# Batch 0's half-way feature: a product with ones before the first chunk in place of one-row products in its first four steps

## Chip, core and metric

One core of a Trainium2 chip runs the kernel. It has TensorE (matrix products; PE, with its weight loads as PEld), VectorE (DVE), ScalarE (ACT), GpSimd (POOL) and SyncE (SP, which here only issues transfers). The metric is the device time of one execution in microseconds (us). All numbers are float32.

## What is computed

The input `x` has 8 batches of 3136 rows by 256 features. The first part is a Fourier mixing: an FFT along the rows, an FFT along the features, and of the result the real part. The second is a gated feed-forward layer with a short convolution:

```python
X = np.fft.fft(x, axis=1); X = np.fft.fft(X, axis=2); x = X.real
h = np.maximum(x @ w_in, 0.0)                       # 256 -> 1024
conv_out = sum over k of conv_w[k] * hp[:, k:k + S] # 3 taps along the rows, h padded by zeros
gate = 1.0 / (1.0 + np.exp(-conv_out))
return h * gate @ w_out                             # 1024 -> 256
```

Cosine and sine tables of the FFT along the rows are an input too. The weights arrive as 64-bit numbers and are narrowed on the chip.

## The kernel before

**The mixing.** The FFT along the rows is made by products with the tables. By symmetry, rows n and S - n and features d and D - d are folded together first (`fold_ops`, VectorE), so that a batch needs half the outputs. For each batch nine small *units* (`units`) multiply the folded rows with the tables: TensorE makes two parts in one PSUM bank, ScalarE copies one part out (`copy`), and VectorE adds and subtracts the two (`fin`). The results are two tables per batch, `PQ[b][0]` (`pt`, the cosine side) and `PQ[b][1]` (`qt`, the sine side), with 128 partitions of features and 1569 columns of frequencies.

**The feature D/2.** Feature 128, the half-way one, is its own mirror image, and its row of the cosine side has no place among the 128 partitions of `pt`. It is kept as a row `er` of 1569 values on one partition. For batch 0 the row comes in two parts. `row()` (L360) fetches the last partition of `qt`, which holds its odd columns, by a transfer. The unit `feature()` (L327) computes the even ones: its `copy` is four ScalarE copies of one row (L345), its `fin` is four GpSimd sums of one row (L353, L354). `flip()` (L364, ScalarE) then changes the sign of every fourth column. `store()` (L368) writes `er` to a row of the DRAM tensor `ed`, and `spread()` (L463) reads it back from there to all 128 partitions, one tile `eb[b, c]` for each chunk `c`; the pool of `eb` has four buffers. For the other batches another route (`Feature`, L374) fills `ed`.

**The weights.** The FFT along the features is put into the weight: `blocks(i)` (L614) multiplies the feature tables `dm` by a quarter `w4[i]` of `w_in` and has ScalarE copy the two results to `G[:, 0]` (cosine side) and `G[:, 1]` (sine side). For quarters 0 and 1 it also makes the one row of weights that belongs to feature D/2, and puts it into partition 0 of the tile `left` (L626, L627). `column(i)` (L631) makes that same row of weights as a column `ge`, one value for each of the 128 output channels of a block.

**The steps.** The 1024 channels are 8 blocks `f` of 128, the 1569 frequencies are 4 chunks `c` (`CUTS`). A step is `(b, c, f)`: 8 x 4 x 8 = 256 steps. For a step,

- `seed` (L660) lets ScalarE write `eb * ge[f]` into the PSUM tile `pa` (L668): the feature D/2. TensorE then adds to it without starting the bank anew.
- `products` (L680) makes `pb` from `G[:, 1]` and `qt`, and adds the product of `G[:, 0]` and `pt` to `pa`. In steps 3 to 19 (`triple`) a third product, of `G[:, 1]` and `qt`, is added to `pa` too.
- `copies` (L691, ScalarE) brings `pb` to SBUF (`nb`); in `triple` steps ScalarE also makes one half of `h` from `pa` (L699).
- `combine` (L704, VectorE) makes `h` (both halves by L713, in `triple` steps one), `first_tap` (L716, ScalarE), `other_taps` (L721, VectorE, L725), `sigmoid` (L734, ScalarE) and `gate` (L740, shared by GpSimd L745 and VectorE L746) follow in later cycles, and `mm2` (L750) multiplies the gated `h` by `w_out` into four PSUM banks `po` that are shared with the blocks and units (`spare`).

In the first four steps, `first(s)` is true (`FIRST = 4`): `seed` does nothing, and `products` adds the feature D/2 by a third TensorE product with one row on each side:

```python
if first(s):
    mm(pa[s][:, 0:n], left[0:1, f, :], er[b][:, ch.k0:ch.k1], False, not triple(s))
```

In steps 4 and 5, each the first seeded one in its `pa` bank, `start_all` (L667) makes a product over all 512 columns of the bank ahead of the seed. There are two `pa` banks, one `pb` bank and one bank `pd` for the units.

**The order.** It is written out by hand. Each engine executes its instructions in the order of the program text and waits in that order. Ahead of the steps come, for batch 0: `keep_on(16)` (L775), 16 products of 256 columns into an unused tile while the folds and the tables are on the way; the four odd units, quarter by quarter; `mend_row(0)` (L229), which scales one row of a table; the units 2, 4, 3, 7, 8, of which number 4 is `feature()`; `flip`, `store`, `spread` of all four chunks; the loads of half of batch 1; `blocks(0)`. SyncE's queue carries the row transfer, the load of `w_out`, the store, the spreads and the loads, in this order. Then, with `products` and `copies` of step 0 done, cycle `t` of the main loop (L901) issues: `sigmoid` of step t-2; a piece of weight narrowing ("first"); `products` and `copies` of step t+1; `combine` of step t; the other piece of the narrowing ("dve"); `seed` of step t+2; `first_tap` of t; `other_taps` of t-1; `gate` of t-2; loads ("load"); `mm2` of t-3; and what is placed at "pe". There, cycles 0, 1 and 2 hold `blocks(1)`, `blocks(2)` and `blocks(3)`, the last two with their columns, and cycles 0 and 1 also `column(0)` and `column(1)`. Narrowing is VectorE work with a power made by ScalarE in between (L525, then L527 on ScalarE, then L539, L540, L533, L543). In cycle 5, `Feature.place` takes the buffer of `er` for other tables, which gathers of 4-byte elements (L418) fill.

Of the kernel before, what the change touches and what calls it, by code (L numbers as in the profile page):

```python
# [9 lines left out]
F32 = mybir.dt.float32  # L10
I32 = mybir.dt.int32
U32 = mybir.dt.uint32
AF = mybir.ActivationFunctionType
# [14 lines left out]


TRIPLE = 3, 20  # L30
FIRST = 4
RC = 56
NQ = 8
CUTS = (0, 384, 768, 1152)
# [4 lines left out]
def kernel(  # L39
# [10 lines left out]
    nc = tc.nc  # L50
    B, S, D = x.shape
    F = moe_w_in.shape[1]
    P = 128
    M = S // 2
    Q4 = S // 4
    NP = Q4 // NQ
# [13 lines left out]
    const = ctx.enter_context(tc.tile_pool(name="const", bufs=1))  # L70
# [4 lines left out]
    ebp = ctx.enter_context(tc.tile_pool(name="ebp", bufs=4))  # L75
# [7 lines left out]
    psa = ctx.enter_context(tc.tile_pool(name="psa", bufs=2, space=PSUM))  # L83
    psb = ctx.enter_context(tc.tile_pool(name="psb", bufs=1, space=PSUM))
    psd = ctx.enter_context(tc.tile_pool(name="psd", bufs=1, space=PSUM))
# [5 lines left out]
    act = nc.scalar.activation  # L91

    def mm(o, l, r, start, stop):
        nc.tensor.matmul(o, l, r, start=start, stop=stop, skip_group_check=True)  # L94

    def spare():

        return pso.tile([P, 2, D], F32, name="po", tag="po").rearrange("p a d -> p (a d)")
# [4 lines left out]
    xh, wt, ea = {}, {}, {}  # L103
# [101 lines left out]
    PQ, eb, er = {}, {}, {}  # L205
# [29 lines left out]
    def mirror_tables(q):  # L235

        for to, of, s in ((2, 1, -1.0), (3, 0, 1.0)):
            for i in range(2):
                act(tabs[1][0:KR, to, q:q + 2, i:HO:2], tabs[1][0:KR, of, q:q + 2, i:HO:2], AF.Copy,
                    scale=-s if i else s)  # L240
# [222 lines left out]
    def spread(b, cs):  # L463

        for c in cs:
            ch = chunks[c]
            eb[b, c] = ebp.tile([P, HN], F32, name="eb", tag="eb")[:, 0:ch.k1 - ch.k0]
            nc.sync.dma_start(out=eb[b, c], in_=ed[b:b + 1, ch.k0:ch.k1].to_broadcast([P, ch.k1 - ch.k0]))
# [31 lines left out]
    chunks = [Chunk(c) for c in range(len(CUTS))]  # L500
    HW = max(c.w for c in chunks)
    HN = max(c.k1 - c.k0 for c in chunks)
    left = const.tile([P, NF, P], F32, name="left")
# [42 lines left out]
    class Weight:  # L546
# [19 lines left out]
        def narrow(self, c0, c1):  # L566
            for f in self.parts(c0, c1):
                f()

    ident = gp.tile([3 * NF, 3 * NF], F32, name="ident", tag="g")  # L570
    make_identity(nc, ident)
    cw24 = gp.tile([3 * NF, 1, P], F32, name="cw24", tag="g")
# [10 lines left out]
    dm = gp.tile([P, 2, 2, P], F32, name="dm", tag="g")  # L583
    N4 = F // 4
    w4 = [win[i // 2][:, :, i % 2 * N4:(i % 2 + 1) * N4] for i in range(4)]
# [24 lines left out]
    G = const.tile([P, 2, F], F32, name="G")  # L610
    ge = const.tile([P, NF], F32, name="ge")
    cw = const.tile([P, 3, NF], F32, name="cw")

    def blocks(i):  # L614


        w = w4[i]
        for g in range(2):
            p = spare()
            for t in range(2):  # L620
                mm(p[:, 0:N4], dm[:, t, g, :], w[:, t], t == 0, t == 1)
            nc.scalar.copy(out=G[:, g, i * N4:(i + 1) * N4], in_=p[:, 0:N4])
        if 2 * i < FIRST:
            p = spare()
            for t in range(2):
                mm(p[0:1, N4:2 * N4], dm[:, t, 1, P - 1:P], w[:, t], t == 0, t == 1)  # L626
            nc.scalar.copy(out=left[0:1, 2 * i:2 * i + 2].rearrange("p f i -> p (f i)"), in_=p[0:1, N4:2 * N4])  # L627
        if i > 1:
            column(i)

    def column(i):  # L631
        w, p = w4[i], spare()
        for m in range(NF // 4):
            for t in range(2):
                mm(p[:, m:m + 1], w[:, t, m * P:(m + 1) * P], dm[:, t, 1, P - 1:P], t == 0, t == 1)
        nc.scalar.copy(out=ge[:, i * NF // 4:(i + 1) * NF // 4], in_=p[:, 0:NF // 4])
# [7 lines left out]
    rows = out.rearrange("b s d -> (b s) d")  # L644
    hs, gs, pa, pb, po, nb = {}, {}, {}, {}, {}, {}

    def start_all(p, l, r):

        mm(p, l, r, True, True)

    def cut(s):
        b, c, f = s
        ch = chunks[c]
        return ch, ch.k1 - ch.k0, slice(f * P, (f + 1) * P)

    def first(s):

        return s[0:2] == (0, 0) and s[2] < FIRST

    def seed(s):  # L660

        b, c, f = s
        ch, n, fs = cut(s)
        pa[s] = psa.tile([P, 512], F32, name="pa", tag="pa")
        if not first(s):
            if s in ((0, 0, FIRST), (0, 0, FIRST + 1)):
                start_all(pa[s].rearrange("p (t n) -> p t n", t=2), dm[:, 0, 0], w4[0])  # L667
            act(pa[s][:, 0:n], eb[b, c], AF.Copy, scale=ge[:, f:f + 1])  # L668

    def triple(s):  # L670

        return s[0] == 0 and TRIPLE[0] <= s[1] * NF + s[2] < TRIPLE[1]

    def row_of(s):
        hs[s] = hp.tile([P, HW], F32, name="h", tag="h")
        w = chunks[s[1]].w
        if chunks[s[1]].zeros:
            nc.gpsimd.memset(hs[s][:, 0:w:w - 1], 0.0)

    def products(s):  # L680
        b, c, f = s
        ch, n, fs = cut(s)
        pb[s] = psb.tile([P, 512], F32, name="pb", tag="pb")
        mm(pb[s][:, 0:n], G[0:P - 1, 1, fs], PQ[b][1][0:P - 1, ch.k0:ch.k1], True, True)
        mm(pa[s][:, 0:n], G[:, 0, fs], PQ[b][0][:, ch.k0:ch.k1], first(s), not first(s) and not triple(s))
        if first(s):
            mm(pa[s][:, 0:n], left[0:1, f, :], er[b][:, ch.k0:ch.k1], False, not triple(s))
        if triple(s):
            mm(pa[s][:, 0:n], G[0:P - 1, 1, fs], PQ[b][1][0:P - 1, ch.k0:ch.k1], False, True)

    def copies(s):  # L691

        ch, n, fs = cut(s)
        p = pb.pop(s)
        nb[s] = nbp.tile([P, 2, HN], F32, name="nb", tag="nb")
        if triple(s):
            act(nb[s][:, 1, ch.cols], p[:, ch.cols], AF.Copy, scale=-2.0)
            row_of(s)
            act(hs[s][:, ch.front], pa[s][:, ch.fcols], AF.Relu)  # L699
        else:  # L700
            for i, cols in enumerate((ch.fcols, ch.cols)):
                act(nb[s][:, i, cols], p[:, cols], AF.Copy, scale=-1.0 if i else 1.0)  # L702

    def combine(s):  # L704

        ch, n, fs = cut(s)
        a, c = pa.pop(s), nb.pop(s)
        if not triple(s):
            row_of(s)
        h = hs[s]  # L710
        for i, (to, cols) in enumerate(((h[:, ch.front], ch.fcols), (h[:, ch.back][:, ::-1], ch.cols))):
            if i or not triple(s):
                nc.vector._custom_dve(TENSOR_ADD_SAT, out=to, in0=a[:, cols], in1=c[:, i, cols],  # L713
                                      s0=BIG, s1=0.0)
# [19 lines left out]
    def sigmoid(s):  # L734

        v, p, r = shares(s)
        for c in (slice(p.start, r.stop), v):
            act(gs[s][:, c], gs[s][:, c], AF.Sigmoid)  # L738
# [33 lines left out]
    taps()  # L772
    idle = psb.tile([P, 512], F32, name="pb", tag="pb")

    def keep_on(n):  # L775

        for _ in range(n):
            mm(idle[:, 0:2 * P], wt[0][1][0:NP, 1, 0], wt[0][1][0:NP, 0, 0:2], True, True)

    begin, us, row, flip, store = units(0)  # L780
    begin()
# [4 lines left out]

    odds = [us[j] for j in (0, 1, 5, 6)]
    w_in[0].narrow(0, 2)
    keep_on(16)
    mirror_tables(0)  # L790
    mend_row(1, half)
    mirror_tables(2)
# [10 lines left out]
                    w_out.load(nc.sync)  # L803
    mend_row(0, half)
    w_in[1].narrow(0, 2)
    for i, u in enumerate(us[j] for j in (2, 4, 3, 7, 8)):
        u.matmuls(0, 1)
        u.copy()
        u.fin()
    flip()  # L810
    store()
    spread(0, range(len(chunks)))
    for f in load_ops(1, 0, nc.sync):
        f()
    blocks(0)
# [5 lines left out]
    def at(cycle, where, fn):  # L821
        side.setdefault((cycle, where), []).append(fn)
# [6 lines left out]
    def shared(cycle, w, c):  # L829
        for where, fn in zip(("first", "dve"), w.parts(c, c + 2, room)):  # L830
            at(cycle, where, fn)

    shared(0, w_in[3], 0)
    for i in (0, 1):
        at(i, "pe", lambda i=i: column(i))
    for cycle, c in ((2, 0), (3, 2), (5, 4), (7, 6)):
        shared(cycle, w_out, c)
    for j, fn in enumerate(load_ops(1, 1, nc.sync)):
# [26 lines left out]
    for b in range(1, B):  # L865
        begin, us, *_ = units(b)
        us = us[0:4] + us[5:]
        c0, n = ends[b], per * b - 3 - ends[b]
# [12 lines left out]
    for b in range(1, B):  # L881
        ops = fold_ops(b)
        c0, n = ends[b - 1], ends[b] - ends[b - 1]
# [12 lines left out]
    n = len(steps)  # L896
    seed(steps[0])
    seed(steps[1])
    products(steps[0])
    copies(steps[0])  # L900
    for t in range(n + LAG):  # L901
        def run(where):
            for fn in side.get((t, where), []):
                fn()
        if 0 <= t - 2 < n:
            sigmoid(steps[t - 2])
        run("first")
        if t + 1 < n:
            products(steps[t + 1])
            copies(steps[t + 1])  # L910
        run("act")
        if t < n:
            combine(steps[t])
        run("dve")
        if t + 2 < n:
            seed(steps[t + 2])
        if t < n:
            first_tap(steps[t])
        if 0 <= t - 1 < n:
            other_taps(steps[t - 1])  # L920
        if 0 <= t - 2 < n:
            gate(steps[t - 2])
        run("load")
        if t >= LAG:
            mm2(steps[t - LAG])
        run("pe")
# [66 lines left out]
```

## Time and profile before

| | |
|---|---|
| time, median of 7 runs | 1214.5 us (1213.68 to 1215.8) |
| the profiled execution: time | 1215.09 us |
| the profiled execution: span of its records | 1213.3 us |
| busy TensorE / weight loads | 1184.0 / 906.7 us |
| busy VectorE / ScalarE / GpSimd | 1119.8 / 881.3 / 373.9 us |
| mean granted clock of TensorE | 0.999 |
| chain that ended last: TensorE, VectorE | 71%, 20% of the span |

The profile is of one execution, so its durations add up to its own span, and the time outside the span is the rest of its 1215.09 us. A row of the timeline gives start and duration in us, the engine (PE is TensorE's products, PEld its weight loads, SPq the transfers that SyncE issues), the line of the program, the operation, the tile written and the tiles read, shapes, a count, and in brackets how long the engine stood idle before it and what released it. Nearly all TensorE work is recorded under line 94, the helper `mm`, so it is told apart by its tiles. One float32 product appears as two records. A row of busy time by stretches gives the stretch, its length, then busy time with the count of instructions for PE, PEld, DVE, ACT and POOL, the granted clock, the share of the transfer engines and GB/s.

### The profile page before, as it was taken

How to read it: one execution, taken by the hardware profiler on the slowest of the kernel's cores; microseconds unless marked ns; L12 is line 12 of the kernel's file. 1: busy time of each engine (PE TensorE's matmuls, PEld its weight loads, DVE VectorE, ACT ScalarE, POOL GpSimd, SP SyncE). 2: the span in 40 equal slices, each digit the busy share in tenths (PEclk: the TensorE clock that was granted, in tenths of full speed). 3: DMA queues.
4: the chain of work that ended last, by engine and by line, in shares of the span. 5: the costliest groups of instructions: out<-in, count | busy, mean ns of one | idle time of the engine just before them, and what ended most of it. 6: DMA issues, size and time to landing. Idle time of an engine off the chain costs nothing.

```text
span 1213.3 us, 15439 instructions
## 1 busy us (share of the span) xinstructions
PE 1184.0 (98%) x4870; PEld 906.7 (75%) x4870; DVE 1119.8 (92%) x1689; ACT 881.3 (73%) x1837; POOL 373.9 (31%) x475
## 2 busy tenths in 40 slices
PE   4999999999999999999999999999999999999998
PEld 3676676777777777777777777777777777777776
DVE  7799999999999899999989999999998988899996
ACT  2477656777777777777777777777777777788884
POOL 5224534243233232424224242332222222222222
PEclk9999999999999999999999999999999999999999
DMA  9522233211131210202021020310001000110000
GB/s 227 190 20 87 81 33 103 61 53 47 34 94 44 67 40 19 89 26 76 31 80 58 1 80 27 94 40 26 27 1 53 31 26 27 46 34 27 26 27 31
DMA packets 70213, 66.30 MB, mean 55 GB/s; under 512 B 28123, under 2 KB 57827, under 8 KB 70131
## 3 DMA queue, kind: packets, MB, share of 16 engines
q1 hardware_dynamic: 64493, 52.18, 15.2%
q0 software_dynamic: 5120, 12.85, 3.4%
q8 instruction: 39, 0.64, 0.2%
q10 hardware_dynamic: 518, 0.28, 0.1%
q14 instruction: 43, 0.35, 0.1%
HBM read 39.53 MB, written 25.74 MB: 54 GB/s over the span
## 4 chain that ended last, share of the span: by engine, by line
PE 71%; DVE 20%; issue 4%; ACT 2%; DMA 1%; DVEq 0%; SPq 0%; ACTq 0%
PE po L94 44%; PE pb L94 10%; PE pa L94 10%; DVE g L725 7%; PE pd L94 6%; DVE h L713 3%; DVE g L746 3%; DVE xh L158 2%; ACT nb L702 1%; DVE xh L169 1%; DVE w L186 1%; DVE w L187 1%; DMA xh<-in_x_dram 0%; ACT g L738 0%; DVE xh L173 0%
## 5 line engine op out<-in xcount | busy, mean ns | idle before, releaser
L94 PE MATMUL po<-wout,g 128*128 128x256 f32 x3072 | 710.1, 381 | 8.1 <-DVE g L746 7.6
L94 PEld LDWEIGHTS po<-wout,g 128*128 128x128 f32 x3072 | 580.1, 190 | 160.5 <-DVE g L746 38.2
L725 DVE SCALAR_TENSOR_TENSOR g<-h,cw,g 128x770 f32<-128x770 f32 (+1 forms) x512 | 548.6, 1072 | 9.3 <-ACT g L719 0.2
L745 POOL TENSOR_TENSOR g<-g,h 128x385 f32<-128x385 f32 (+1 forms) x256 | 234.1, 915 | 760.7 <-ACT g L738 494.0
L738 ACT ACTIVATE g<-g 128x385 f32<-128x385 f32 (+2 forms) x512 | 244.2, 527 | 190.2 <-DVE g L725 189.7
L702 ACT ACTIVATE nb<-pb 128x386 f32<-128x386 f32 (+2 forms) x478 | 210.8, 493 | 86.1 <-PE pb L94 85.0
L713 DVE CUSTOM_DVE_ANT_0 h<-pa,nb 128x386 f32<-128x386 f32 (+2 forms) x495 | 257.1, 560 | 1.0 <-PE pa L94 1.0
L719 ACT ACTIVATE g<-h,cw 128x770 f32<-128x770 f32 (+1 forms) x256 | 243.2, 950 | 0.2 <-DVE h L713 0.2
L94 PE MATMUL pb<-qt,G 127*128 127x387 f32 (+2 forms) x512 | 212.7, 496 | 0.0
L94 PE MATMUL pa<-pt,G 128*128 128x387 f32 (+2 forms) x512 | 211.8, 494 | 0.0
L668 ACT ACTIVATE pa<-eb,ge 128x387 f32<-128x387 f32 (+2 forms) x252 | 151.5, 601 | 1.2 <-ACT ft L459 0.6
L94 PEld LDWEIGHTS pa<-pt,G 128*128 128x128 f32 x512 | 96.8, 189 | 73.6 <-issue 18.2
L746 DVE TENSOR_TENSOR g<-g,h 128x385 f32<-128x385 f32 (+1 forms) x256 | 146.2, 571 | 0.9 <-ACT g L738 0.9
L94 PE MATMUL pd<-tab,w 98*128 98x196 f32 (+3 forms) x448 | 126.7, 374 | 0.0
L133 POOL DMA_INDIRECT xh<-in_x_dram,idx x64 | 105.9, 1655 | 13.3 <-issue 9.2
L94 PEld LDWEIGHTS pb<-qt,G 127*128 127x128 f32 x512 | 93.9, 190 | 18.2 <-issue 1.9
L94 PEld LDWEIGHTS pd<-tab,w 98*128 98x128 f32 (+1 forms) x448 | 84.7, 191 | 12.3
L765 ACT COPY os<-po 128x256 f32<-128x256 f32 x196 | 57.6, 395 | 7.8 <-PE po L94 4.6
L158 DVE TENSOR_TENSOR xh<-xh 98x1020 f32<-98x1020 f32 (+1 forms) x32 | 40.7, 1278 | 3.3 <-DMA xh<-in_x_dram,idx 3.3
L169 DVE TENSOR_TENSOR xh<-xh 98x1024 f32<-98x1024 f32 (+1 forms) x32 | 41.3, 1292 | 0.1
L188 POOL COPY w<-xh 98x4 f32<-98x4 f32 (+1 forms) x32 | 20.3, 633 | 28.0 <-DVE xh L169 14.8
L291 DVE TENSOR_TENSOR qt<-as,pd 128x197 f32<-128x197 f32 (+1 forms) x14 | 7.2, 517 | 20.3 <-ACT as L287 20.3
(117 smaller groups left out, 385.4 us busy)
## 6 DMA issues: line engine op xcount, KB each, us to landing
out_dram<-os SPq DMA_DIRECT2D x192, 128.0 KB
xh<-in_x_dram SPq DMA_DIRECT2D x16, 784.0 KB
eb<-ed SPq DMA_DIRECT2D x16, 193.5 KB
tab<-dft_seq_dram SPq DMA_DIRECT2D x4, 589.5 KB
raw<-in_moe_w_in_dram SPq DMA_DIRECT2D x4, 512.0 KB
raw<-in_moe_w_out_dram SPq DMA_DIRECT2D x1, 2048.0 KB
eb<-ed SPq DMA_DIRECT2D x8, 209.0 KB
eb<-ed SPq DMA_DIRECT2D x8, 193.0 KB
```

The lines of the kernel that those rows point to most:

```text
L94: nc.tensor.matmul(o, l, r, start=start, stop=stop, skip_group_check=True)
L133: nc.gpsimd.indirect_dma_start(out=xh[b, h][0:NP, 7 - m].rearrange("p q d -> p (q d)"), out_offset=None, in_=bass.AP(tensor=x.tensor, offs ...
L158: vt(a[:, :, :, 1:D], a[:, :, :, 1:D], r[:, :, :, D - 1:0:-1], op=ALU.add)
L668: act(pa[s][:, 0:n], eb[b, c], AF.Copy, scale=ge[:, f:f + 1])
L702: act(nb[s][:, i, cols], p[:, cols], AF.Copy, scale=-1.0 if i else 1.0)
L713: nc.vector._custom_dve(TENSOR_ADD_SAT, out=to, in0=a[:, cols], in1=c[:, i, cols], s0=BIG, s1=0.0)
L719: act(gs[s], hs[s][:, 0:n], AF.Copy, scale=cw[:, 0, s[2]:s[2] + 1])
L725: stt(out=g, in0=h[:, k:k + n], scalar=cw[:, k, f:f + 1], in1=g, op0=ALU.mult, op1=ALU.add)
L738: act(gs[s][:, c], gs[s][:, c], AF.Sigmoid)
L745: gt(g[:, p], g[:, p], h[:, p], op=ALU.mult)
L746: vt(g[:, v], g[:, v], h[:, v], op=ALU.mult)
L765: nc.scalar.copy(out=osb[:, j % 2], in_=pt[:, j % 2])
```

## The change

The feature D/2 of chunk 0 reaches all partitions by a product: a row of 128 ones (`one`) as the stationary side and `er` as the moving side, into the bank `pd`, from where ScalarE copies it to `eb[0, 0]`. All steps are then seeded alike; `first`, `FIRST`, `start_all`, the one-row products and the one-row weights in `left` are gone. `column(0)` moves ahead of `blocks(0)` and `column(1)` to just after step 0's copies. The unit `feature()` goes first among the last five, with `flip`, `store` and the spread of chunks 1 to 3 directly behind it. `keep_on` now makes 8 products of 512 columns, six into the unused tile and one into each of the two `pa` banks.

```diff
+    one = const.tile([1, P], F32, name="one")
+    nc.gpsimd.memset(one, 1.0)
     ident = gp.tile([3 * NF, 3 * NF], F32, name="ident", tag="g")
...
-        if 2 * i < FIRST:
-            p = spare()
-            for t in range(2):
-                mm(p[0:1, N4:2 * N4], dm[:, t, 1, P - 1:P], w[:, t], t == 0, t == 1)
-            nc.scalar.copy(out=left[0:1, 2 * i:2 * i + 2].rearrange("p f i -> p (f i)"), in_=p[0:1, N4:2 * N4])
         if i > 1:
             column(i)
...
         pa[s] = psa.tile([P, 512], F32, name="pa", tag="pa")
-        if not first(s):
-            if s in ((0, 0, FIRST), (0, 0, FIRST + 1)):
-                start_all(pa[s].rearrange("p (t n) -> p t n", t=2), dm[:, 0, 0], w4[0])
-            act(pa[s][:, 0:n], eb[b, c], AF.Copy, scale=ge[:, f:f + 1])
+        act(pa[s][:, 0:n], eb[b, c], AF.Copy, scale=ge[:, f:f + 1])
...
-        mm(pa[s][:, 0:n], G[:, 0, fs], PQ[b][0][:, ch.k0:ch.k1], first(s), not first(s) and not triple(s))
-        if first(s):
-            mm(pa[s][:, 0:n], left[0:1, f, :], er[b][:, ch.k0:ch.k1], False, not triple(s))
+        mm(pa[s][:, 0:n], G[:, 0, fs], PQ[b][0][:, ch.k0:ch.k1], False, not triple(s))
...
-    def keep_on(n):
-
-        for _ in range(n):
-            mm(idle[:, 0:2 * P], wt[0][1][0:NP, 1, 0], wt[0][1][0:NP, 0, 0:2], True, True)
+    def keep_on(banks):
+
+        for p in banks:
+            mm(p.rearrange("p (s q d) -> p s q d", s=2, q=2), wt[0][1][0:NP, 1, 0], wt[0][1][0:NP, 0:2, 0:2],
+               True, True)
...
-    keep_on(16)
+    keep_on([idle] * 6)
+
+    keep_on([psa.tile([P, 512], F32, name="pa", tag="pa") for _ in range(2)])
...
-    for i, u in enumerate(us[j] for j in (2, 4, 3, 7, 8)):
+    for i, u in enumerate(us[j] for j in (4, 2, 3, 7, 8)):
         u.matmuls(0, 1)
         u.copy()
         u.fin()
-    flip()
-    store()
-    spread(0, range(len(chunks)))
+        if i == 0:
+            flip()
+            store()
+            spread(0, range(1, len(chunks)))
+
+    n = chunks[0].k1
+    p = psd.tile([P, 512], F32, name="pd", tag="pd")
+    mm(p[:, 0:n], one, er[0][:, 0:n], True, True)
+    eb[0, 0] = ebp.tile([P, HN], F32, name="eb", tag="eb")[:, 0:n]
+    nc.scalar.copy(out=eb[0, 0], in_=p[:, 0:n])
+    column(0)
     for f in load_ops(1, 0, nc.sync):
         f()
     blocks(0)
...
-    for i in (0, 1):
-        at(i, "pe", lambda i=i: column(i))
...
     copies(steps[0])
+    column(1)
     for t in range(n + LAG):
```

More of the change, by code (lines that the diff above doesn't have):

```diff
@@ L30 @@
 TRIPLE = 3, 20
-FIRST = 4
 RC = 56
@@ L645 @@
     hs, gs, pa, pb, po, nb = {}, {}, {}, {}, {}, {}
-    def start_all(p, l, r):
-        mm(p, l, r, True, True)
     def cut(s):
@@ L654, in cut @@
         return ch, ch.k1 - ch.k0, slice(f * P, (f + 1) * P)
-    def first(s):
-        return s[0:2] == (0, 0) and s[2] < FIRST
     def seed(s):
```

## The prediction

> **What bounds the kernel now.** I read the page first, then the opening in order of time, then busy time by stretches, because the diff touches nothing after the first chunk of batch 0. On the page TensorE is busy for 98% of the span and VectorE for 92%, so a change is worth what it moves the engine that ends last in its own stage. Each row of the opening is a start, a duration, the engine and the operation:
>
> ```profile
> 34.79 0.79 SPq L362 DMA_DIRECT2D er<-qt  x1
> ...
> 38.68 0.55 POOL L353 TENSOR_TENSOR er<-as 1x197 f32<-1x197 f32 x1 [10.95 <-ACT as L345]
> ...
> 41.14 0.60 POOL L354 TENSOR_TENSOR er<-as 1x196 f32<-1x196 f32 x1
> ...
> 42.42 0.93 ACT L366 ACTIVATE er<-er 1x392 f32<-1x392 f32 x1
> ...
> 43.62 0.52 PEld L94 LDWEIGHTS po<-win,dm 128*1 128x1 f32 x4 [0.33 <-ACT G L622]
> ...
> 44.58 0.92 PE L94 MATMUL pb<-qt,G 127*128 127x386 f32 x2
> ...
> 45.33 0.81 PE L94 MATMUL pa<-pt,G 128*128 128x386 f32 x2
> ...
> 46.07 0.91 PE L94 MATMUL pa<-er,left 1*128 1x386 f32 x2
> ...
> 46.91 0.92 PE L94 MATMUL pb<-qt,G 127*128 127x386 f32 x2
> ```
>
> Durations overlap in the pipeline, so I cost TensorE by the distance between starts. From 35.08 (after a table scaling) TensorE is never idle: four units, the blocks, step 0, step 1 follow without a gap. Now ScalarE and VectorE at the end of that stretch, in two answers:
>
> ```profile
> 59.07 0.16 ACT L636 COPY ge<-po 128x2 f32<-128x2 f32 x1 [0.73 <-PE po L94]
> 59.25 1.28 ACT L738 ACT_TABLE_LOAD   x1
> 60.54 0.94 ACT L738 ACTIVATE g<-g 128x385 f32<-128x385 f32 x2
> 61.38 0.71 ACT L527 ACTIVATE wout<-wout,low 128x512 int32<-128x512 int32 x1
> ```
> ```profile
> 62.12 0.69 DVE L533 SCALAR_TENSOR_TENSOR wout<-raw,wout 128x512 int32<-128x512 int32 x1 [4.44 <-ACT wout L527]
> ```
>
> ScalarE waits for the last column product on TensorE; then come the table load, the first sigmoid and a power for a weight, and VectorE has stood 4.44 us for that power. What follows is a race:
>
> ```profile
> 70.00:80.00 10.00, 10.00 (x42) 7.63 (x41) 9.82 (x15) 6.89 (x13) 2.89 (x6) 1.00 0.03 9
> 80.00:90.00 10.00, 10.00 (x40) 7.32 (x39) 9.86 (x16) 6.84 (x13) 2.92 (x8) 1.00 0.12 20
> 90.00:100.00 10.00, 10.00 (x40) 7.39 (x39) 9.93 (x14) 6.98 (x14) 3.61 (x4) 1.00 0.29 94
> 100.00:110.00 10.00, 9.36 (x37) 6.63 (x35) 9.93 (x11) 9.17 (x26) 8.92 (x8) 1.00 0.46 139
> ```
>
> The columns after the length are busy time of PE, PEld, DVE, ACT, POOL, then granted clock. Both engines are full until about 100; from there TensorE has holes and VectorE none, until the PE rows of the chain take over at about 145. So what counts is when VectorE is let go at 62.12: it has no idle time worth the name from there to 145, and its work is not changed by the diff. TensorE only has to arrive no later.
>
> **What TensorE loses and gains ahead of 59.07.** Removed: the one-row product of steps 0, 1 and 2, 46.91 - 46.07 = 0.84 each, 2.52 in all; the one-row weights of two blocks, 44.58 - 43.62 = 0.96 each, 1.92. Added: one product with ones, of the same shape as the removed one-row product, 0.84. The two columns are only moved (0.9 each, from 52.13 to 53.04 for the first), still ahead of the sigmoid. Net 2.52 + 1.92 - 0.84 = 3.60 us less. The fourth row product (0.84) and the two 512-wide starting products (62.83 - 61.96 = 0.87 and 0.86) lie behind 59.07, where TensorE only needs to keep up: I cost them at nothing. The cover is VectorE's full rows above; without it they would be worth 2.57 more.
>
> **Two new holes.** The one-row weights ran while ScalarE copied the second half of G. Without them the next product waits for that copy. In the block of 51.17 (not shown) the one-row part starts at 51.17 and the copy ends at 51.28 + 0.37 = 51.65, which is 0.48; the weight load of 0.19 that can start only then makes it 0.67, and I take 0.70. It happens ahead of step 0 and ahead of step 2. Step 1 has a column between, and the single pb bank is free before that column ends. Loss 1.40, gain 3.60 - 1.40 = **2.2 us**.
>
> **The queue of ScalarE, walked through.** The feature unit goes first and `flip` follows at once, so ScalarE stands at `flip` with four unit copies behind it. The feature matmuls end near 35.9, four copies of 0.33 end at 37.3, GpSimd's four sums take 41.74 - 38.68 = 3.06 from 37.1, to 40.2. They need the transfer of the row: the trace's packets of it (three of 2092 bytes) run at 36.4 to 36.6. `flip` (0.93) ends near 41.2, the product with ones can start when TensorE is through the units at 41.80, as before, so no wait there. The unit copies run 41.1 to 42.4, and VectorE's eight results (0.36 apart) end at 44.3 in place of 43.50: 0.8 late. Seven narrowing operations later, L525 is at 48.4 (47.58 before), the power L527 at 48.8, the two copies of step 1 end at 50.2, the new seed of step 2 (L668, 0.59, starts 0.5 apart) at 50.7, the first tap at 51.6. The second G copy of that block is due at 51.9 by TensorE's own count. Thus the 0.8 is hidden with 0.3 to spare, and every microsecond that `flip` is later than that costs one. The seeds of steps 0 and 1 and the 0.5 copy of the spread row lie where ScalarE waits for TensorE. Seeds of steps 2 and 3 wait for `combine` two steps back, as all later seeds do; behind them stands the first tap, which waits for a VectorE result of that same step anyway.
>
> **Other edits, at nothing.** The warming products read 16 x 256 columns before and 8 x 512 after, the same 4096; they end at 26.1 where the first table product begins, so they are on the path. The trace shows half speed at first (four passes of 256 per microsecond until 22, seven after 23); with equal columns that is zero, bounds -0.2 to +0.4 for where a longer pass meets the change. The memset of `one` on GpSimd: starts 0.04 apart, ahead of the gathers that everything waits for, up to 0.04. SyncE gets three spreads instead of four, earlier. The spread tiles now rotate: batch 1's third one takes the buffer of chunk 3, which is read until step 31, so SyncE stands about two steps (some 9 us) with a load of batch 3 behind it; that load is used over six steps later, which hides it. The 4-byte gathers, at 61.31 until now, come free with `er` some 15 us earlier and meet only loads that nobody needs before 80.
>
> **Sum.** The profiled execution took 1215.09 us with a span of 1213.3; the median of the seven is 1214.5, 0.6 below. Span 1213.3 - 2.2 = 1211.1, execution 1212.9, median **1212.3**. From the unknowns above (holes of 0.5 to 1.0 each, ScalarE's spare of 0.3 gone) this case has its own range of 1.4 to 2.9 us gain, 1211.6 to 1213.1. A difference of about 0.2%, 2.4 us, is what a measurement of this kernel can tell from no change; the sum lies just inside.
>
> [...] Row first: the hole of TensorE before 35.08 is 0.88 us, with granted clock 1.00, and the unit after it runs at the pace of the units before; 100 to 110 has 0.64 of holes at 1.00. [...]
>
> **Rivals.**
> 1. *TensorE alone decides.* If the weights of the next product are fetched so that the holes are 0.1 to 0.2 each, or VectorE gets back part of what it lost to late inputs: 3.6 less 0.0 to 0.5, 1210.9 to 1211.4. For it: no hole of this kind after a G copy is in the trace; against it: those weights are G itself. 0.22.
> 2. *The wait moves to `flip`.* GpSimd's sums share the time with VectorE's narrowing; if `flip` ends at 43 instead of 41.2, the ones product, the four copies and VectorE's chain are 1.8 later, 0.3 of it covered: gain 0.7; at 43.7 it is nothing. 1213.8 to 1214.5. Against it: sums and narrowing overlap today as well, at 3.06. 0.09.
> 3. *Slower: the clock drops in the opening.* If a hole of 0.7 sends TensorE back to half speed for as long as at the start (16.06 to 22.4, 6.4 us), each loses 3.2 us of work: two cost 6.4, net +4.2, 1218.7; from one such drop on (+1.0) the gain is gone. Against it: the row of 0.88. 0.16.
>
> **How the numbers follow.** The forecast has 0.53; about a third of it (0.18) lies beyond 2.4 us. Faster: 0.18 + 0.22 = 0.40. Same: 0.35 + 0.09 = 0.44. Slower: 0.16. The range runs from below rival 1 by half a microsecond, for scatter, to above the zero of rival 2 by 0.9, where rival 3 begins: 1210.4 to 1215.4; rival 3's greater part is left out.
>
> **What would show it.** Right: no one-row `pa` rows; the table load near 57.1; VectorE's L533 released near 59.9; holes of about 0.7 on TensorE before the first and third `pb`; TensorE waiting for VectorE's gates between 70 and 100, where today it doesn't; the stretch after 145 as before. Wrong: `flip` ending after 41.6, L533 still near 62, passes of twice the length between 46 and 57, or a release at 59.9 that is given back before 145, which would mean that VectorE was not the one to count.

## The result and the profile after

The changed kernel took 1211.53 us in the median of 15 runs (1209.77 to 1214.29), the kernel before 1214.35 of 36. The ratio is 0.9977, interval 0.997 to 0.9984: faster by 0.23%, 2.8 us. Forecast were 1212.3 us and a range of 1210.4 to 1215.4. The profiled execution took 1213.61 us with a span of 1211.8, only 1.5 below the span of before. Most of this difference between 2.8 and 1.5 is a stretch at half clock in this one execution, shown next.

First the opening of the changed kernel in order of time: the sign change (`flip`, now L365), the first and the last of GpSimd's sums, and the product with ones.

```profile
37.87 0.92 ACT L365 ACTIVATE er<-er 1x392 f32<-1x392 f32 x1 [0.74 <-DMA er<-qt]
...
37.98 1.00 POOL L352 TENSOR_TENSOR er<-as 1x197 f32<-1x197 f32 x1 [10.39 <-DMA er<-qt]
...
40.62 1.06 POOL L353 TENSOR_TENSOR er<-as 1x196 f32<-1x196 f32 x1
...
41.45 0.91 PE L93 MATMUL pd<-er,one 1*128 1x386 f32 x2
```

`flip` does not wait for the sums: both are let go by the transfer of the row, and `flip` starts 0.11 us before the first sum. Next TensorE from the blocks to the third step:

```profile
43.20 3.66 PE L93 MATMUL po<-win,dm 128*128 128x256 f32 x8
47.33 0.92 PE L93 MATMUL pb<-qt,G 127*128 127x386 f32 x2 [0.46 <-issue]
48.08 0.81 PE L93 MATMUL pa<-pt,G 128*128 128x386 f32 x2
48.73 0.95 PE L93 MATMUL po<-dm,win 128*128 128x1 f32 x8
...
53.27 0.92 PE L93 MATMUL pb<-qt,G 127*128 127x386 f32 x2 [0.46 <-ACT G L622]
```

The one-row products are gone, and the two forecast holes are there, 0.46 us each. But the first block takes 3.66 us, where a block of the same eight records further on takes 1.89. Busy time by stretches tells why; the column after the five engines is the granted clock:

```profile
43.00:44.00 1.00, 1.00 (x6) 0.91 (x6) 1.00 (x5) 0.16 (x1) 0.83 (x1) 0.64 0.70 256
44.00:45.00 1.00, 1.00 (x3) 0.73 (x3) 0.93 (x4) 0.00 (x0) 0.70 (x2) 0.50 0.51 123
45.00:46.00 1.00, 1.00 (x4) 0.82 (x3) 0.96 (x2) 0.37 (x1) 0.70 (x2) 0.50 0.65 159
46.00:47.00 1.00, 0.86 (x3) 0.19 (x1) 0.93 (x3) 0.10 (x1) 1.00 (x3) 0.66 0.93 213
...
70.00:80.00 10.00, 9.72 (x38) 7.16 (x39) 9.86 (x17) 7.50 (x16) 3.22 (x8) 1.00 0.08 21
...
100.00:110.00 10.00, 9.00 (x36) 6.32 (x35) 9.93 (x12) 8.86 (x30) 7.44 (x7) 1.00 0.47 141
```

TensorE was given half its clock from 43.3 to 46.7 (the trace's clock record: 3.413 us at 0.5); it had not been idle since 34.82. The row of 70 to 80 shows the other forecast sign: TensorE (9.72) now waits while VectorE (9.86) is as full as it was. The release at the end of the opening, on ScalarE and VectorE:

```profile
57.39 0.16 ACT L632 COPY ge<-po 128x2 f32<-128x2 f32 x1 [0.41 <-PE po L93]
57.57 1.28 ACT L721 ACT_TABLE_LOAD   x1
```
```profile
60.44 0.69 DVE L532 SCALAR_TENSOR_TENSOR wout<-raw,wout 128x512 int32<-128x512 int32 x1 [2.71 <-ACT wout L526]
```

VectorE is released 62.12 - 60.44 = 1.68 us earlier. Paired row by row in the two traces, its gates (L746 before, L729 after) are 1.68 earlier at the first, 1.65 at the 45th and 1.58 at the last one. All 256 pairs lie between 1.3 and 1.8. What the opening gives is kept to the end.

### The profile page after: what moved, and what is told of

Read it like the earlier page. It is cut to its first block, busy times and chain, and to the rows that moved or that the text cites. A ratio compares the mean times of both kernels' runs of the same rounds, so it can differ in the third digit from the quotient of the medians.

```text
span 1211.8 us, 15374 instructions
## 1 busy us (share of the span) xinstructions
PE 1179.3 (97%) x4836; PEld 900.4 (74%) x4836; DVE 1120.3 (92%) x1689; ACT 882.1 (73%) x1840; POOL 374.2 (31%) x476
## 4 chain that ended last, share of the span: by engine, by line
PE 71%; DVE 20%; issue 4%; ACT 2%; POOL 1%; DMA 1%; DVEq 0%; SPq 0%; POOLq 0%; ACTq 0%
PE po L93 44%; PE pb L93 11%; PE pa L93 10%; DVE g L708 7%; PE pd L93 6%; DVE h L696 3%; DVE g L729 3%; DVE xh L157 2%; ACT nb L685 1%; DVE xh L168 1%; DVE w L185 1%; DVE w L186 1%; POOL xh L132 1%; DMA xh<-in_x_dram 0%; ACT g L721 0%
## 5 line engine op out<-in xcount | busy, mean ns | idle before, releaser
L729 DVE TENSOR_TENSOR g<-g,h 128x385 f32<-128x385 f32 (+1 forms) x256 | 146.2, 571 | 0.9 <-ACT g L721 0.9
```

The costliest lines, as they stand in the source:

```text
L729: vt(g[:, v], g[:, v], h[:, v], op=ALU.mult)
```

## Experiments

The theory formed on this (A): the gain is the shorter road of TensorE to the column product ahead of the table load, about 3 us, less a half-clock window that only some executions have. Rivals: the slow window belongs to the change and is always there (B); ScalarE's and VectorE's own order sets the release (C); and rival 1 of the prediction, TensorE alone decides.

A run's median is uncertain by about 1 us against another's. The profile of one execution gives a sharper measure: the time from the first table product on TensorE (`po<-tab,w`, at 26.08 before) to the release of VectorE's weight step (62.12 before). Everything up to the first table product is the same in all kernels but for the form of the warming products and the memset of `one`.

| kernel | warming products, us | first table product to release, us | half clock in the opening | median, us | ratio to before (interval) |
|---|---|---|---|---|---|
| before | 10.02 | 36.04 | none | 1214.35 | |
| changed | 10.37 | 34.16 | 43.3 to 46.7 | 1211.53 | 0.9977 (0.997 to 0.9984) |
| changed, again | 10.23 | 34.32 | 42.2 to 45.6 | 1211.91 | 0.9979 (0.997 to 0.9988) |
| feature unit second | 9.51 | 33.13 | none | 1211.48 | 0.9975 (0.9966 to 0.9984) |
| before, feature unit first | 8.96 | 36.19 | none | 1214.54 | 1.0003 (0.9994 to 1.0012) |
| dense work behind column(2) | 10.02 | 33.11 | none | 1211.76 | 0.9977 (0.9968 to 0.9987) |
| dense work ahead of blocks(2) | 10.11 | 34.77 | none | 1213.14 | 0.9994 (0.9985 to 1.0003) |
| column(0) behind blocks(0) | 9.11 | 32.90 | none | 1211.22 | 0.9977 (0.9968 to 0.9986) |
| 16 narrow warming products | 8.85 | 32.75 | none | 1211.42 | 0.9979 (0.997 to 0.9988) |
| second, and column behind | 10.26 | 32.78 | none | 1210.89 | 0.9975 (0.9966 to 0.9985) |
| three more thin products | 10.41 | 37.72 | 43.0 to 49.8 | 1213.83 | 0.9998 (0.9989 to 1.0007) |
| three more dense products | 10.43 | 34.73 | none | 1212.96 | 0.9990 (0.9981 to 0.9999) |

**The changed kernel again.** No edit.

> The changed kernel, unaltered, once more, to see a second execution in detail. Theory A (TensorE's road to the column product of cycle 1 sets VectorE's release; a half-clock window of 3.4 us lies in the opening of some executions only): median gain 2.5 to 3.1 us again, and single executions fall into a group with granted clock 1.00 near 1211.2 and a group below it 1.5 to 2 us above. If the profiled one has no half-clock window between 40 and 60, VectorE's weight step (L532) is released near 58.8 in place of 60.44. Theory B (the slow blocks at 43 to 47 are part of the change itself, every time): the window is there again at the same place and the release is at 60.4 again.

The gain came again (2.5 us), and so did the window, one microsecond earlier. Taken alone this speaks for B. But of the 17 listed executions of the first measurement, the ten with a mean granted clock of 1.00 lie between 1209.77 and 1211.84, and the five with 0.998 or less between 1212.07 and 1214.29: not every execution has it. The two runs with dense work below settle it.

**The feature unit second.**

```diff
-    for i, u in enumerate(us[j] for j in (4, 2, 3, 7, 8)):
+    for i, u in enumerate(us[j] for j in (2, 4, 3, 7, 8)):
...
-        if i == 0:
+        if i == 1:
             flip()
```

> The changed kernel with the unit of feature D/2 second instead of first among the last five units, flip, store and spread behind it as before. Theory A: the first unit must again wait for both scaled table rows (0.5 us) and the sums end a little later: 0.5 to 0.9 us slower than the changed kernel. Theory C (the order of ScalarE's queue, with flip early, gave the gain): no loss at all, or over 1.5 us if flip now holds up copies.

A miss: no loss (1211.48 against 1211.91, measured together), and 33.13 us in the profile. TensorE does wait again for the second scaled row (the hole before the units is 0.90, 0.44 in the changed kernel), yet it gets this back at the third step. VectorE's rows say how. In this run, with the sums at 37.88 to 40.94, the seven narrowing operations of the second quarter start at 35.50 and are over at 39.84, in 4.34 us; of them:

```profile
37.61 0.43 DVE L538 TENSOR_SCALAR raw<-raw 128x512 int32<-128x512 int32 x1
...
38.07 0.90 DVE L539 SCALAR_TENSOR_TENSOR raw<-raw 128x512 f32<-128x512 uint32 x1
```

With the feature unit first (the run with dense work behind column(2), whose text is the changed kernel's up to there) the sums run at 36.90 to 40.38, the narrowing takes 35.93 to 40.85, 4.92 us, and the same two operations:

```profile
38.24 0.67 DVE L538 TENSOR_SCALAR raw<-raw 128x512 int32<-128x512 int32 x1
...
38.95 0.97 DVE L539 SCALAR_TENSOR_TENSOR raw<-raw 128x512 f32<-128x512 uint32 x1
```

So in these profiles VectorE's operations over 128 partitions took longer beside the sums of one row. The profile of the changed kernel has the last three narrowing operations of a quarter (L538, L539, L542) both ways: 0.43, 0.69 and 0.69 us at 29.23 to 31.11, where GpSimd had nothing to do, and 0.65, 0.90 and 0.97 at 38.62 to 41.20, beside the sums at 37.98 to 41.68. In the two profiles quoted above the order that saves TensorE 0.5 us costs VectorE about as much (4.92 - 4.34 = 0.58), and the two effects cancel.

**The kernel before, feature unit first.**

```diff
-    for i, u in enumerate(us[j] for j in (2, 4, 3, 7, 8)):
+    for i, u in enumerate(us[j] for j in (4, 2, 3, 7, 8)):
```

> The kernel before with one edit: the unit of feature D/2 goes first among the last five; flip, store and spread stay where they were. Theory A: only the wait for the second scaled table row is saved, 0.4 to 0.6 us faster than before. If the order alone carried the gain, 1.5 us or more; if the order is worth nothing, 0.

Nothing gained, 1.0003. TensorE is through its units 0.5 to 0.7 us earlier after the first table product, and then stands:

```profile
40.12 2.92 PE L94 MATMUL po<-win,dm 128*128 128x256 f32 x12 [0.56 <-ACT as L287]
```

The releaser shown is the last unit's copy, which ends at 40.07; by the rotation of the four banks the block writes into the bank of the first unit, which VectorE's second result frees at 40.02. Which of the two it was stays open. Either way, in the kernel before, where TensorE is never idle at this place, another engine was less than a microsecond behind it. The order alone is not the gain, so C falls in this form.

**Dense work behind, and ahead of, the releasing product.** Two products over 512 columns, results unused, in cycle 1: once directly behind column(2), once ahead of blocks(2).

```diff
+    def dense():
+        for _ in range(2):
+            mm(spare().rearrange("p (t n) -> p t n", t=2), dm[:, 0, 0], w4[0], True, True)
...
     for i in (1, 2, 3):
         at(i - 1, "pe", lambda i=i: blocks(i))
+    at(1, "pe", dense)          # the run ahead of blocks(2) has this line above the loop
```

> The changed kernel with two more TensorE products of 512 columns (about 0.87 us each, 1.74 in all, results unused) in cycle 1 directly behind column(2), that is behind the product that releases ScalarE's table load. Theory A: TensorE has spare time there until about 97 us, so the loss is 0 (within 0.4). Rival 1 of the prediction (TensorE alone decides): 1.7 us slower than the changed kernel.

> The changed kernel with the same two extra products of 512 columns (1.74 us), but ahead of blocks(2) in cycle 1, in front of the product that releases ScalarE's table load. Theory A: 1.5 to 1.8 us slower than the changed kernel, VectorE's release that much later, and the shift kept to the end. Theory C (ScalarE's or VectorE's own queue sets the release): 0 to 0.5 slower.

The release behind, then ahead; the first table product starts at 25.71 and 25.48:

```profile
58.82 0.69 DVE L532 SCALAR_TENSOR_TENSOR wout<-raw,wout 128x512 int32<-128x512 int32 x1 [2.03 <-ACT wout L526]
```
```profile
60.25 0.69 DVE L532 SCALAR_TENSOR_TENSOR wout<-raw,wout 128x512 int32<-128x512 int32 x1 [3.76 <-ACT wout L526]
```

Behind: 1211.76, no loss. Ahead: 1213.14, and the release 34.77 - 33.11 = 1.66 us later; counted from the first table product, the gates are 1.66 later at the first and 2.07 at the last. The same 1.74 us of TensorE cost nothing on one side of the column product and all of it on the other. That is theory A's core and the end of rival 1. The median of the second run says it less sharply: six of its 11 executions have a mean clock of 0.998 or less, and the other five lie at 1212.11 to 1213.59. That what the change took away behind that point (the fourth row product, the two starting products, 2.57 us) is worth nothing fits the first run, which had 1.74 us of such work; the removal itself was not tried alone.

Both kernels have the changed kernel's own instructions up to the first copies behind blocks(1), and neither has a half-clock window. So B falls: the window is a matter of the execution. In the first of them, which thus shows the undisturbed opening:

```profile
42.69 1.97 PE L93 MATMUL po<-win,dm 128*128 128x256 f32 x8
...
45.12 0.92 PE L93 MATMUL pb<-qt,G 127*128 127x386 f32 x2 [0.46 <-DVE win L529]
...
51.65 0.92 PE L93 MATMUL pb<-qt,G 127*128 127x386 f32 x2 [1.04 <-ACT G L622]
```

The block takes 1.97, the release comes 33.11 after the first table product. The undisturbed gain is 36.04 - 33.11 = 2.93 us, and a window takes 34.16 - 33.11 = 1.05 of it (1.21 in the repetition). It takes less than the 1.7 by which the block is longer, because the second hole, 1.04 here, shrinks to 0.46: there ScalarE and VectorE are late, and a late TensorE doesn't wait for them.

**column(0) behind blocks(0).**

```diff
-    column(0)
     for f in load_ops(1, 0, nc.sync):
         f()
     blocks(0)
+    column(0)
```

> The changed kernel with column(0) moved from ahead of blocks(0) to directly behind it. Theory A: the column product covers most of the 0.46 us in which TensorE waits for the second copy of G, so 0.3 to 0.45 us faster than the changed kernel; the product with ones and the column no longer stand side by side, so a half-clock window in the opening may become rarer, worth up to 0.5 more in the median. Against: the seeds of steps 0 and 1 now also wait for the column's copy; if that wait decides, 0 or up to 0.3 slower.

The first hole is gone but for 0.12 ahead of the `pa` product, 32.90 us, 0.21 better than 33.11; the second hole grows to 1.22, as VectorE is no earlier. The forecast of 0.3 to 0.45 was too high, and the medians (1211.22 against 1211.53 and 1211.91, not measured together) don't separate the two. None of its 11 executions has a mean clock below 0.999.

**Warming products in the old width.**

```diff
-            mm(p.rearrange("p (s q d) -> p s q d", s=2, q=2), wt[0][1][0:NP, 1, 0], wt[0][1][0:NP, 0:2, 0:2],
-               True, True)
+            for s in range(2):
+                mm(p[:, s * 2 * P:(s + 1) * 2 * P], wt[0][1][0:NP, 1, 0], wt[0][1][0:NP, s, 0:2], s == 0, True)
```

> The changed kernel with the warming products in the old width: 16 of 256 columns, two halves in each bank, in place of 8 of 512. If the width makes the warming longer (10.37 us in the changed kernel's profile against 10.02 before), 0.3 us faster than the changed kernel; if that was only where the clock's change of speed falls in the one execution, 0 within 0.2.

8.85 us here, but 9.11, 9.51 and 10.02 in kernels with the wide form, and 8.96 and 10.02 in the two with the narrow form of before: the same products vary by 1.2 to 1.3 us between executions. The clock records go with it: the first one, of full clock, begins 3.75 us after the first warming product here, and up to 6.99 us after it in the other profiles (6.10 before, 6.87 in the first profile of the changed kernel). Until then the products run at about half the later pace: in the profile of before three or four records of 256 columns fall in each microsecond from 17 to 22, seven from 23 to 25, and the clock record begins at 22.16. The length of the warming products less half of the time until that record is 6.93 to 6.97 us in all twelve profiles. The median, 1211.42, shows no effect of the width. The release at 32.75 goes with a late transfer in this one execution: counted from the first table product, the sums started 1.6 us later than in the run of 33.11, they overlapped the narrowing less (4.12 us for it, not 4.92), and the second hole was 0.46.

**Both moves at once.** The edits of the feature unit second and of column(0) behind blocks(0) together.

> The changed kernel with both moves at once: the unit of feature D/2 second instead of first (so that GpSimd's sums overlap less of VectorE's narrowing) and column(0) behind blocks(0) (so that it covers the first wait for a copy of G). Theory A with VectorE as the second limit: each part has room now, 0.5 to 0.9 us faster than the changed kernel, VectorE's release about 32.5 us after the first table product (33.1 in the runs without a half-clock window). If TensorE alone counted: 0.15 slower to 0.1 faster, since the moved unit costs TensorE the 0.5 that the column gains.

Release at 32.78, 1210.89 us, the lowest median of all. The release is 0.33 earlier than the 33.11 of the undisturbed opening, the median 0.64 below the changed kernel's 1211.53; forecast were 0.5 to 0.9. By ratio it is 0.9975 against 0.9977, so that the times do not prove a gain over the changed kernel. None of the 21 executions of the two kernels with column(0) behind blocks(0) has a mean clock below 0.999, against 8 of the 28 listed of the changed kernel. That fits the expectation that the window becomes rarer when the product with ones and the column are apart; it is a count and does not show the cause.

**Three more thin, three more dense products.**

```diff
+    for _ in range(3):     # dense; the thin run repeats the next line four times instead
+        mm(p[:, 0:n], dm[:, 0, 0], win[0][:, 0, 0:n], True, True)
     mm(p[:, 0:n], one, er[0][:, 0:n], True, True)
```

> The changed kernel with the product of ones made four times instead of once: three more products of one row, 0.84 us each, 2.5 in all. Theory A with thin work as what brings the half-clock window (products with one row or one column use little of TensorE): 2.0 to 2.5 us for the time itself and, on top, a half-clock window near 42 to 48 in the profile and lower mean clocks in most executions: 3 to 4 us slower than the changed kernel. Against (the window does not depend on what the products fill): 2.0 to 2.5 us and as many low clocks as before.

> The changed kernel with three more products of the same 386 columns ahead of the product of ones, but with 128 rows and 128 columns of weights (results unused). The time on TensorE is the same as in the run with thin products, 2.0 to 2.5 us. Theory A with thin work: no half-clock window in the profile's opening and hardly a low clock among the executions, so 1 us or more faster than the run with three more thin products. Against: as slow as that run.

The thin run, then the dense run, busy time by stretches:

```profile
44.00:46.00 2.00, 2.00 (x8) 1.22 (x6) 1.90 (x5) 0.48 (x1) 1.28 (x5) 0.50 0.60 192
46.00:48.00 2.00, 2.00 (x8) 1.73 (x8) 1.90 (x4) 0.16 (x1) 0.00 (x0) 0.50 0.70 153
```
```profile
44.00:46.00 2.00, 2.00 (x14) 1.61 (x13) 1.90 (x5) 0.64 (x2) 1.69 (x4) 1.00 0.48 169
46.00:48.00 2.00, 1.54 (x7) 1.02 (x6) 1.90 (x4) 1.14 (x3) 0.17 (x4) 1.00 0.34 79
```

TensorE is full from 42 to 46 in both, and full again from 46 to 48 in the thin run. With thin products, which fill 41.14 to 46.51 there, the clock is halved for 6.8 us, twice the 3.413 of the first profile; all 11 executions have a mean clock of 0.998 or less. With dense ones there is no window in the opening, and 6 of 11 have 0.999. But the dense run still has the change's own two thin products side by side, as the changed kernel has, and they ran at full clock:

```profile
43.47 0.91 PE L93 MATMUL pd<-er,one 1*128 1x386 f32 x2
44.31 1.05 PE L93 MATMUL po<-dm,win 128*128 128x1 f32 x8
```

The same pair ran at full clock in the profiles of the unit second, of both dense kernels above and of the narrow warming products. So in this comparison thin products go with a low clock more often (11 of 11 executions against 5 of 11). What decides it for a single execution stays open: the changed kernel has 8 of 28, and the run with dense work ahead of blocks(2) has 6 of 11. The thin run is 0.87 us slower in the median, and its release 37.72 - 34.73 = 2.99 later; of that, about 0.4 is the thin products' own time (0.84 against 0.70 each). Expected was 1 us or more, and hardly any low clock in the dense run, where five lie at 0.997 or 0.998 and are no slower than the six others (1212.96 against 1213.32 in the median); those may have their dips elsewhere, as the profile of before has one from 206.5 to 209.9 us (3.413 us at 0.5) and the first one of the changed kernel a second from 1210.6 to the end of the span, after its last product. Expected was also that the thin run would be 3 to 4 us slower than the changed kernel. By the medians it is 1.9 to 2.3 slower, which is about the time of the products alone; the profiled execution, 1216.76, is the slowest of its 11, and the others lie at 1213.52 to 1214.76.

## Why the prediction was right, point by point

- *What counts.* That VectorE's release decides, that the gain is kept to the end, and that TensorE's work behind the table load is free: right, by the paired gates, the row of 70 to 80 and the two dense runs.
- *The sum.* 2.2 forecast, 2.93 undisturbed, 1.9 in an execution with a window (36.04 - 34.16), 2.8 in the median. The error is in three places. The first is a part not seen at all: the feature unit uses only the first scaled table row, so behind the first table product the units of the changed kernel end 0.56 earlier. The second: a step without its row product is 1.40 long (47.33 to 48.73), not 1.49, three times; the three columns take 2.51 in the undisturbed opening and took 2.62 before, where the prediction had them unchanged. The third is the holes, 0.46 and 1.04 undisturbed in place of 0.70 and 0.70: almost right in sum and wrong one by one. Together 2.2 + 0.56 + 0.27 + 0.11 - 0.10 = 3.04, near the 2.93; most of the rest is the product with ones, 0.93 long there and not 0.84.
- *The queue of ScalarE.* This step failed. It held that `flip` waits for the sums and four copies stand behind it. `flip` needs only the odd columns, which the transfer brings, and the sums write only the even ones. The transfer in turn was taken as landed when its packets are seen, near 36.6 (in the trace of before they start at 36.2 to 36.5). In the changed kernel its last packet started at 37.21, and the waiters were released 0.66 later, at 37.87, 2.9 after the issue at 35.01; in the experiments it was 2.1 to 4.0. So the sums ended at 41.7 in place of 40.2. TensorE had begun the product with ones at 41.45, since that product reads the first chunk's columns alone, and the third of the four sums completes these, at 40.66. The conclusion (VectorE somewhat late, little of it visible) held by luck; its cause is the slower narrowing next to the sums.
- *Warming products at nothing, -0.2 to +0.4.* 10.37 against 10.02 in the two first profiles; the experiments show 8.85 to 10.43 whatever the kernel, in step with the start of the clock record (3.75 to 6.99 us after the first of these products). The bounds were too narrow for one execution, and zero is what the medians show.
- *Rival 3, the clock.* The clock does drop in the opening of some executions, at a smaller price and not for the reason given. No run shows the term it was added up from, a hole that sends TensorE back to half speed for 6.4 us (3.2 lost by each): holes of up to 1.22 us brought no window in any of these openings. Further on, a hole of 1.93 us in the profile of before, up to 206.32, was followed by a window of 3.413, and one of 1.94 in the first profile of the changed kernel, up to 204.65, by none. In the three profiles with a window in the opening, TensorE had been on products with one row or one column for nearly all of the 1.7 to 1.9 us before it. Two such products side by side were in the change, and the prediction costed them by their length alone; that they are the cause was not shown, as five profiles have the same pair at full clock. The price at the release is 1.05 to 1.21 in the two of them with a single window there, not 3.2 for each hole. The executions of the changed kernel with a mean clock of 0.998 or less are 2.0 us (first measurement) and 1.3 us (again) slower in the median than its others, somewhat more than the release shows. The sign of passes of twice the length between 46 and 57 nearly came: the window of the first profile ended at 46.7.
- *Chances.* Just past the line of 0.2%, as a third of the main case allowed.

## What to carry to other kernels

Before costing an edit, find the one instruction whose lateness is passed on, and ask of each removed product on which side of it the product lies: the same 1.7 us was worth 1.7 or nothing. Read from the code which elements a waiting instruction really shares with the one ahead, columns and all, before putting it into a queue of waits. And where an edit is worth 0.2%, compare the executions inside their profiles from a common event on: here the warming products (1.6 us) and a half-clock window (1.05 to 1.21) together move a single execution by almost as much as the edit.

## What was not expected of the hardware

Each of these is what the profiles and times of the runs above show, and no more than that.

- The clock was halved for 3.413 us while TensorE was busy (43.3 to 46.7 in the first profile of the changed kernel), 1.7 to 1.9 us after products with one row or one column had begun, and for 6.8 us in the profile with three more thin products, where such products fill 41.14 to 46.51; with dense products of the same number of columns in place of the added ones the clock was 1.00 from 40 to 54. The same pair of thin products also ran at full clock in five profiles, so that they may raise the chance of a window and don't settle it (a mean clock of 0.998 or less in 11 of 11 executions with the added thin products, in 5 of 11 with the dense ones).
- Beside GpSimd's sums over a single partition, VectorE's operations over 128 partitions took longer: 0.65 us in place of 0.43, 0.90 and 0.97 in place of 0.69 in the first profile of the changed kernel.
- Equal warming products took 8.85 to 10.43 us from one execution to the next; the clock record of full clock began 3.75 to 6.99 us after the first of them.
